# Forgetting attention with two FFN layers on one core: queries' and keys' high parts made in place, copies of the output and the normalising moved within a step

## The chip, the cores and the metric

The program runs on one core of a Trainium2 chip. Times are device microseconds of one execution. Before the change the median of three runs is 1031.77 us (1030.31 to 1033.46). One execution was taken by the hardware profiler; it took 1022.97 us, of which 1021.2 us are the span from its first to its last instruction.

## The reference

Everything is float32. For 4 batches of 8 heads with 576 positions and 64 columns a head:

```python
scores = scale * q @ k.T                       # scale = 1/8
cum = cumsum(log(clip(f, 1e-4, 1)), axis=-1)
scores = where(causal, -1e9, scores + cum[:, :, :, None] - cum[:, :, None, :])
attn = exp(scores - max(scores)); attn = attn / (sum(attn) + 1e-9)
x = (attn @ v) laid out as 2304 tokens x 512
h = x @ w_in;  x = (h - tanh(h)) @ w_out       # first FFN, 512 -> 2048 -> 512
h = x @ w_in2; out = (h * sigmoid(h)) @ w_out2 # second FFN
```

## The kernel before

Float32 accuracy is reached by splitting an operand into a high part that TensorE takes exactly and the rest, `hi` and `lo`, and by summing hi·hi, hi·lo and lo·hi.

**Stages.** The attention of 16 pairs of heads comes first and takes some 237 us of the span; the two FFN layers follow. Of the change only the attention is touched.

**Tiles and steps.** Each pair has nine score tiles: four of the first head (128, 256, 384 and 512 keys), one tile with the last 64 queries of both heads (576 keys), four of the second head. The 144 tiles are numbered through, and one loop goes over a step number n. In step n TensorE transposes tile n - 9, scores tile n + 2 and does a part of the products with the values of an older pair. VectorE takes the row minimum of tile n (`least`), ScalarE the exponential of tile n - 1 (`expo`). Results of a transposition are copied by ScalarE (`evac_a`) and VectorE (`evac_b`). Every third step VectorE sums three rows' sums (`guard`) and GpSimd scales the three finished tiles by the reciprocals (`normalise`). `collect_a`, `collect_b` and `collect_0` copy a head's output from PSUM into x. The order of the calls in the loop (lines 759 to 782) is the order of the instructions on each engine, since the schedule is written by hand. Engines run ahead of each other as far as their semaphores let them.

**The operands of the scores.** Two buffers serve the pairs in turn, pair p the buffer p % 2. A buffer is two tiles, `kqa` and `kqb`, each with one slot for the first and one for the second head. From the third pair on a head's scores are two matmuls: in `kqa` rows 0 to 63 hold hi of keys and queries, rows 64 to 127 hold lo of the keys beside hi of the queries; in `kqb` rows 0 to 63 hold hi of the keys beside lo of the queries, rows 64 to 67 the decay (`dec`). The matmul on `kqb` thus reads the decay rows too. (The first two pairs use the buffers in a plain form, with four matmuls a tile.)

**How they get there.** `load_kq` brings the raw keys and queries of both heads, 128 rows. `split` makes hi (GpSimd the keys, VectorE the queries) and lo (GpSimd, four pieces) in two tiles of their own, `kqhi` and `kqlo`, of which there is one each. `place` then moves them by DMA from SyncE's queue, ten copies of 64 rows a pair and two small ones for the decay. `prep` (line 676) says in which step of a pair each of these calls is issued. SyncE takes its DMAs strictly in order: a wait of one holds back all behind it. A copy's completion is told by a semaphore.

**Beside it** the weights of the FFN are loaded on the same queue (`wload`, in steps 27, 36, 45, 54, 90, 99, 135 and 137) and decoded by all of ScalarE, VectorE and GpSimd.

Of the kernel before, what the change touches and what calls it, by code (L numbers as in the profile page):

```python
# [8 lines left out]
F32R = mybir.dt.float32r  # L9
# [5 lines left out]
P = 128  # L15
B, H, S, D = 4, 8, 576, 64
# [9 lines left out]
K0, Q0, Z1, Q1, W = 64, 64 + S, 64 + S + 512, 128 + S + 512, 192 + S + 512  # L26
RAW = W - K0
# [13 lines left out]
def forgetting_attention_two_ffn(  # L41
# [12 lines left out]
    nc = tc.nc  # L54
# [9 lines left out]
    def rd(ap):  # L64
        return ap.bitcast(F32)
# [140 lines left out]
    for l in range(2):  # L206
        c0 = 0
        for si, nch in enumerate(SETS[l]):
# [8 lines left out]
            for j, n in enumerate(span):  # L217
                a, b = (nxt * NSTAGE * (j + i) // len(span) for i in range(2))
# [109 lines left out]
    def attention():  # L328
        with ExitStack() as actx:
# [4 lines left out]
            def pool(stack, name, bufs=1, **kw):  # L334
                return stack.enter_context(tc.tile_pool(name=name, bufs=bufs, side="right", **kw))
# [9 lines left out]
            rq = pool(earlier, "rq")  # L345
            ps_s = pool(early, "ps_s", 3, space=PSUM)

            NP = B * NPAIR
            raw, vraw, kqs, vals = {}, {}, {}, {}
            kqt = []  # L350
            for i in range(2):
                ta = kp.tile([P, 2, W], F32R, name=f"kqa{i}")
                tb = kp.tile([P, 2, W], F32R, name=f"kqb{i}")
                kqt.append((ta, tb))
# [14 lines left out]
            plain = [[t[:, j, K0:W] for t, j in ((ta, 0), (ta, 1), (tb, 0))] for ta, tb in kqt]  # L369
# [12 lines left out]
            def sub(out, a, b):  # L382
                nc.gpsimd.tensor_tensor(out, a, b, ALU.subtract)

            def split(p, j):
                if p not in kqs:
                    kqs[p] = plain[p][0:2] if p < 2 else [
                        rq.tile([P, RAW], F32R, tag=tag, name=f"{tag}{p}") for tag in ("kqhi", "kqlo")
                    ]
                hi, lo = kqs[p]  # L390
                if j == 0 and p > 1:
                    nc.gpsimd.tensor_scalar(hi[:, 0:S], raw[p][:, 0:S], 1.0, 1.0, ALU.mult, ALU.mult)
                elif j < 2:
                    c = KQ if j == 0 else slice(S, RAW)
                    (nc.vector.tensor_copy if p else nc.scalar.copy)(hi[:, c], raw[p][:, c])
                else:
                    c0, c1 = ((0, 288), (288, S), (S, S + 320), (S + 320, RAW))[j - 2]
                    sub(lo[:, c0:c1], raw[p][:, c0:c1], rd(hi[:, c0:c1]))

            def split_last(p, j):  # L400

# [24 lines left out]
            def place(p, j):  # L426


                ta, tb = (rd(t) for t in kqt[p % 2])
                if j == 2:  # L430
                    src = dec[2 * p:2 * p + 2].rearrange("h r w -> r h w")
                    if p < 4:

                        nc.vector.memset(tb[64:68, :, Z1:Q1], 0.0)
                    nc.sync.dma_start(out=tb[64:68, :, K0:Z1], in_=src[:, :, 0:S + 512])
                    nc.sync.dma_start(out=tb[64:68, :, Q1:W], in_=src[:, :, S + 512:2 * S])
                    return
                for h in range(2):
                    a = rd(kqs[p][j][64 * h:64 * h + 64])
                    if j == 0:  # L440
                        nc.sync.dma_start(out=ta[0:64, h, K0:W], in_=a)  # L441
                        nc.sync.dma_start(out=ta[64:128, h, Q0:W], in_=a[:, S:RAW])  # L442
                        nc.sync.dma_start(out=tb[0:64, h, K0:Q0], in_=a[:, 0:S])
                    else:
                        nc.sync.dma_start(out=ta[64:128, h, K0:Q0], in_=a[:, 0:S])
                        nc.sync.dma_start(out=tb[0:64, h, Q0:W], in_=a[:, S:RAW])

            def prep_v(p, j):
                r = vraw[p].rearrange("p h (c d) -> p c h d", d=D)[:, :, 0, :]
# [82 lines left out]
            def guard(n):  # L532
                sm = rowsum[n // 3] = small.tile([P, 3], F32, tag="sm", name=f"sm{n}")
                nc.vector.tensor_reduce(sm, sums[:, n // 3 % 5], axis=AX.X, op=ALU.add)  # L534

            def normalise(n):
                sm = rowsum.pop(n // 3)
                nc.vector.reciprocal(sm, sm)  # L538
                for j in range(3):
                    pt, w, _ = ptile[tiles[n + j]]  # L540
                    nc.gpsimd.tensor_scalar(pt[:, :w], pt[:, :w], sm[:, j:j + 1], 1.0, ALU.mult, ALU.mult)  # L541
# [7 lines left out]
            def transposes(t):  # L549
                p, h, i = t  # L550
                pt = ptile[t][0] if i == 4 else ptile.pop(t)[0]
                tp = ps_t.tile([P, 4, P], F32, tag="t", name=f"t{p}_{h}_{i}")
                nch = min(i + 1, 4)
                for c in range(nch):
                    nc.tensor.transpose(tp[:, c, :], pt[:, c * P:c * P + P], ident)  # L555
                if i == 4:
                    tps[t] = tuple(
                        [(tp[:, :, 64 * g:64 * g + 64], lambda a: cols(a, 512, 4, 64))] for g in range(2)
                    )
                    return  # L560
                a = [(tp[:, 0:nch, :], lambda a: cols(a, P * i, nch, P))]
                tps[t] = (a, []) if h == 0 else ([], a)
                if (h, i) == (1, 0):

                    t5, o = tp[:, 1, :], 448 * 4 + 512
                    nc.tensor.transpose(t5, ptile.pop((p, 2, 4))[0][:, 512:640], ident)
                    for g in range(2):
                        tps[t][g].append((t5[:, 64 * g:64 * g + 64], lambda a: a[:, o:o + 64]))

            def evac_a(t):  # L570
                ptf = ptfs[t[0] % 2]
                for src, dst in tps[t][0]:
                    nc.scalar.copy(dst(pth), src)  # L573
                for src, dst in tps[t][1]:
                    if t[2] >= 3:
                        nc.scalar.copy(dst(ptf), src)
# [77 lines left out]
            for j in range(2, 6):  # L654
                split(0, j)
            split_last(0, 1)
            dec = dram.tile([BH, 4, 2 * S], F32, name="dec")
# [12 lines left out]
            for a in pt4:  # L670
# [3 lines left out]
            scores(tiles[1])  # L674

            prep = {
                -8: [(load_kq, None)], -5: [(split, 0), (split, 1)], -4: [(split, 2)], -3: [(split, 3)],
                -2: [(split, 4), (place, 2), (place, 0)], -1: [(split, 5), (place, 1)],
                10: [(prep_v, 0)], 12: [(prep_v, 1)], 15: [(load_v, None)],
            }  # L680
            due = {}
# [1 line left out]
            def later(n, fn, *a):  # L683
                due.setdefault(max(n, 0), []).append((fn, a))

            def run(n, *fns):
                for fn, a in due.get(n, []):
                    if fn in fns:
                        fn(*a)

            for p in range(NP - 1):
                for k, items in prep.items():
                    for fn, j in items:
                        if fn is prep_v:
                            later(9 * p + k, fn, p + 1, j)
                        elif j is not None:
                            if p:
                                later(9 * p + k, fn, p + 1, j)
                        elif p + 2 < NP and (p or fn is load_v):
                            later(9 * p + k, fn, p + 2)  # L700

            parts = (
                ([(0, 0), (64, 0), (64, 1)], [(64, 2), (64, 3), (64, 4)]),
# [2 lines left out]
            for n, (p, h, i) in enumerate(tiles):  # L706
# [3 lines left out]
                if (h, i) in ((2, 4), (1, 3)):  # L710
                    h = int(h == 1)
# [13 lines left out]
            def has(n):  # L725
                return 0 <= n < N
# [32 lines left out]
            for n in range(N + LAG + 9):  # L759
                if has(n - LAG):  # L760
                    transposes(tiles[n - LAG])
                if has(n + 2) and tiles[n + 2][2] < 4:
                    scores(tiles[n + 2])
                run(n, scores_tail, values)
                run(n, collect_a)
                if has(n - LAG - 1):
                    evac_a(tiles[n - LAG - 1])
                if has(n - 1):
                    expo(n - 1)
                run(n, collect_b)  # L770
                run(n, collect_0)
                if has(n - LAG - 2):
                    evac_b(tiles[n - LAG - 2])
                if n % 3 == 2 and has(n - 5):
                    guard(n - 5)
                if has(n):
                    least(tiles[n])
                if n % 3 == 2 and has(n - 5):
                    normalise(n - 5)
                run(n, load_kq, load_v, split, place, prep_v)  # L780
                for fn, *a in ahead.get(n - N, []):
                    fn(*a)
# [4 lines left out]
    with tc.manual_schedule():  # L787
        attention()
        for n in range(len(steps) + HL):
            if n > HL:  # L790
                front(n)
            if n >= HL:
                project(n - HL)
# [39 lines left out]
```

## Time and profile before

| what | us |
|---|---|
| median of three runs | 1031.77 |
| profiled execution | 1022.97 |
| its span | 1021.2 |
| span up to 237.3 us (attention) | 237.3 |
| span from there (FFN layers) | 783.9 |
| TensorE busy in these two parts | 211.1 and 780.1 |
| mean busy share of the 16 DMA engines in these two parts | 0.78 and 0.12 |

A busy TensorE is modelled, so what tells more is how far apart the same work of one pair and the next begins. In the rows below PE is TensorE's matmuls, PEld its weight loads, DVE VectorE, ACT ScalarE, POOL GpSimd, and SPq SyncE's queue, on which an instruction's time is that of issuing the DMA, not of its transfer. In the chain of waits a piece named DMA lasts from the start of the issue to the landing that somebody waited for.

### The profile page before, as it was taken

Reading aid. Unit: us, or ns where it says so; the run is one execution under the profiler, and the core shown is the slowest. Engines: PE = TensorE matmul, PEld = TensorE weight load, DVE = VectorE, ACT = ScalarE, POOL = GpSimd, SP = SyncE. Lnnn points to the kernel's source line nnn. Section 1 sums busy time; section 2 is a strip of 40 time slices with the busy share of each in tenths; the row PEclk is TensorE's granted clock in tenths of the full one; section 3 lists DMA queues with packets and bytes.
Section 4 is the critical chain, followed back from the end, with each engine's and each line's share of the span. In section 5 each row is a group of like instructions: output and inputs, shape, how many; then the busy total and the mean of one; then the engine's idle time right before and its main releaser. Section 6 shows DMA issues by size and latency. Waiting matters only on the chain.

```text
span 1021.2 us, 14016 instructions
## 1 busy us (share of the span) xinstructions
PE 991.2 (97%) x4944; PEld 828.5 (81%) x4944; DVE 597.1 (58%) x1385; ACT 492.8 (48%) x1094; POOL 202.1 (20%) x288
## 2 busy tenths in 40 slices
PE   5989989999999999999999999999999999999998
PEld 4777777877898888988888888888888888888887
DVE  6677788878686544757466674443453456633323
ACT  4678788885355342434343444343344334433222
POOL 8677888975000000000000000000000000000000
PEclk9999999999999999999999999999999999999999
DMA  5899999812221101111011220110110111001111
GB/s 154 231 256 258 226 234 268 211 49 84 82 83 42 42 1 42 62 63 42 1 42 49 77 83 1 42 41 21 63 42 1 42 42 42 1 1 42 42 41 62
DMA packets 28181, 81.78 MB, mean 80 GB/s; under 512 B 4368, under 2 KB 4368, under 8 KB 28080
## 3 DMA queue, kind: packets, MB, share of 16 engines
q1 hardware_dynamic: 28104, 80.88, 27.0%
q8 instruction: 39, 0.64, 0.3%
q14 instruction: 30, 0.25, 0.1%
q10 hardware_dynamic: 8, 0.02, 0.0%
HBM read 49.39 MB, written 5.31 MB: 54 GB/s over the span
## 4 chain that ended last, share of the span: by engine, by line
PE 85%; DMA 5%; ACT 3%; SPq 2%; POOL 2%; DVE 2%; issue 1%; DVEq 0%; POOLq 0%; ACTq 0%
PE a L315 39%; PE h L256 38%; PE out_t L600 3%; DMA kqb<-kqhi 2%; PE t L555 2%; PE s L473 2%; DMA vraw<-v 1%; ACT p L527 1%; DMA kqb<-kqlo 1%; SPq L441 1%; POOL p L541 1%; PE s L477 1%; SPq L442 1%; ACT pth L573 1%; PE s L476 1%
## 5 line engine op out<-in xcount | busy, mean ns | idle before, releaser
L256 PE MATMUL h<-xh,wh 128*128 128x512 f32 (+1 forms) x640 | 237.2, 371 | 0.0
L256 PE MATMUL h<-xl,wh 128*128 128x512 f32 (+1 forms) x640 | 235.5, 368 | 0.0
L256 PE MATMUL h<-xh,wl 128*128 128x512 f32 (+1 forms) x640 | 235.5, 368 | 0.0
L278 DVE TENSOR_TENSOR gl<-g,gh 128x512 fp32r<-128x512 f32 (+1 forms) x158 | 101.6, 643 | 101.8 <-ACT gh L274 99.8
L274 ACT CAST gh<-g 128x512 fp32r<-128x512 f32 (+1 forms) x160 | 92.6, 579 | 95.9 <-DVE g L271 93.4
L256 PEld LDWEIGHTS h<-xh,wh 128*128 128x128 f32 x640 | 120.7, 189 | 21.1 <-issue 0.7
L256 PEld LDWEIGHTS h<-xl,wh 128*128 128x128 f32 x640 | 120.7, 189 | 21.0 <-issue 0.7
L256 PEld LDWEIGHTS h<-xh,wl 128*128 128x128 f32 x640 | 120.6, 188 | 20.0
L315 PE MATMUL a<-gh,wh 128*128 128x512 f32 (+1 forms) x320 | 117.9, 369 | 0.0
L315 PE MATMUL a<-gl,wh 128*128 128x512 f32 (+1 forms) x320 | 117.8, 368 | 0.0
L315 PE MATMUL a<-gh,wl 128*128 128x512 f32 (+1 forms) x320 | 117.7, 368 | 0.0
L315 PE MATMUL a<-wh,gh 128*128 128x512 f32 x288 | 112.2, 390 | 0.0
L315 PE MATMUL a<-wl,gh 128*128 128x512 f32 x288 | 112.2, 390 | 0.0
L315 PE MATMUL a<-wh,gl 128*128 128x512 f32 x288 | 112.0, 389 | 0.0
L273 ACT ACTIVATE g<-h 128x512 f32<-128x512 f32 (+1 forms) x80 | 44.4, 555 | 113.6 <-PE h L256 98.5
L244 DVE TENSOR_TENSOR xl<-y,xh 128x512 fp32r<-128x512 f32 (+1 forms) x60 | 37.4, 638 | 96.6 <-ACT xh L242 96.6
L242 ACT CAST xh<-y 128x512 fp32r<-128x512 f32 (+1 forms) x60 | 34.2, 580 | 104.8 <-PE h L256 103.1
L527 ACT ACTIVATE p<-p,mn 128x128 f32<-128x128 f32 (+3 forms) x128 | 72.3, 565 | 9.7 <-DVE mn L511 4.8
L541 POOL TENSOR_SCALAR p<-p,sm 128x128 f32<-128x128 f32 (+3 forms) x128 | 69.9, 558 | 22.9 <-DVE sm L538 10.4
L555 PE MATMUL t<-ident,p 128*128 128x128 f32 x320 | 59.6, 285 | 12.7 <-DVE sm L534 9.2
L244 DVE TENSOR_TENSOR xl<-x,xh 128x512 fp32r<-128x512 f32 (+1 forms) x56 | 34.5, 634 | 62.2 <-ACT xh L242 62.2
L315 PEld LDWEIGHTS a<-gh,wh 128*128 128x128 f32 x320 | 60.3, 189 | 10.4 <-ACT x L611 0.4
(127 smaller groups left out, 1690.8 us busy)
## 6 DMA issues: line engine op xcount, KB each, us to landing
raw<-w_in SPq DMA_DIRECT2D x32, 512.0 KB
raw<-w_out SPq DMA_DIRECT2D x32, 512.0 KB
kqraw<-kq SPq DMA_DIRECT2D x16, 608.0 KB
kqa<-kqhi SPq DMA_DIRECT2D x28, 304.0 KB
vraw<-v SPq DMA_DIRECT2D x16, 320.0 KB
out<-ob SPq DMA_DIRECT2D x18, 256.0 KB
kqa<-kqhi SPq DMA_DIRECT2D x28, 160.0 KB
kqb<-kqlo SPq DMA_DIRECT2D x28, 160.0 KB
```

Source lines behind the costliest of these rows:

```text
L242: nc.scalar.copy(hi[:, :n], src[:, k, t0:t0 + n])
L244: eng.tensor_tensor(lo[:, :n], src[:, k, t0:t0 + n], rd(hi[:, :n]), ALU.subtract)
L256: nc.tensor.matmul(hp[:, :n], w[:, k * P:k * P + P], m[:, :n], start=(k == 0 and r == 0), stop=(k == NKT - 1 and r == 2),)
L273: nc.scalar.activation(g[:, :n], hp[:, :n], AF.Silu)
L274: nc.scalar.copy(gh[:, :n], g[:, :n])
L278: eng.tensor_tensor(gl[:, :n], g[:, :n], rd(gh[:, :n]), ALU.subtract)
L315: nc.tensor.matmul(dst, w, m, start=(first and r == 0), stop=(last and r == 2))
L473: nc.tensor.matmul(s[:, :n], a[:, q], b[:, 0:n], start=r == 0, stop=r == 3)
L527: nc.scalar.activation(pt[:, :w], pt[:, :w], AF.Exp, bias=mn, scale=-1.0, accum_out=sums[:, n // 3 % 5, n % 3, 0:1],)
L541: nc.gpsimd.tensor_scalar(pt[:, :w], pt[:, :w], sm[:, j:j + 1], 1.0, ALU.mult, ALU.mult)
L555: nc.tensor.transpose(tp[:, c, :], pt[:, c * P:c * P + P], ident)
L600: nc.tensor.matmul(dst, w, pt[:, 448 * c + a:448 * c + q1], start=(c == 0 and r == 0), stop=(c == last and r == len(terms) - 1),)
```

## The change

There are three parts.

- **Copies of the output.** In a step `collect_a` and `collect_b` go behind `evac_a`, `expo`, `evac_b`, `guard` and `least`.
- **Normalising.** The reciprocal goes into `guard`, directly behind the sum; the scaling on GpSimd is issued one step later.
- **Operands.** hi is written by `split` directly into slot 0 of `kqa`, all 128 rows, where the first head's 64 rows are in place. lo of the queries goes into slot 0 of `kqb`; lo of the keys goes into one tile `klo`. `place` has eight copies instead of ten, now in three groups: four copies of hi, then the two of `klo`, then two more of queries; the second group overwrites rows that the first one reads, and the third frees the rows into which the decay goes, which is now last. Splits and copies of the third and fourth pair are issued three steps later, since these replace buffers in plain form.

```diff
             def split(p, j):
-                if p not in kqs:
-                    kqs[p] = plain[p][0:2] if p < 2 else [
-                        rq.tile([P, RAW], F32R, tag=tag, name=f"{tag}{p}") for tag in ("kqhi", "kqlo")
-                    ]
-                hi, lo = kqs[p]
+                ta, tb = kqt[p % 2]
+                if p > 1:
+                    hi, lo = ta[:, 0, K0:W], (klo, tb[:, 0, Q0:W])
+                else:
+                    hi, lo = plain[p][0], (plain[p][1][:, 0:S], plain[p][1][:, S:RAW])
...
             def place(p, j):
...
+                moves = (
+                    ((ta[top, 1, K0:W], ta[end, 0, K0:W]), (ta[end, 1, qs], ta[end, 0, qs]),
+                     (tb[top, 1, kk], ta[end, 0, kk]), (tb[top, 0, kk], ta[top, 0, kk])),
+                    ((ta[end, 1, kk], rd(klo[end])), (ta[end, 0, kk], rd(klo[top]))),
+                    ((tb[top, 1, qs], tb[end, 0, qs]), (ta[end, 0, qs], ta[top, 0, qs])),
+                )
+                if j < 3:
+                    for a, b in moves[j]:
+                        nc.sync.dma_start(out=a, in_=b)
                     return
-                for h in range(2):
-                    a = rd(kqs[p][j][64 * h:64 * h + 64])
-                    if j == 0:
-                        nc.sync.dma_start(out=ta[0:64, h, K0:W], in_=a)
-                        nc.sync.dma_start(out=ta[64:128, h, Q0:W], in_=a[:, S:RAW])
-                        nc.sync.dma_start(out=tb[0:64, h, K0:Q0], in_=a[:, 0:S])
-                    else:
-                        nc.sync.dma_start(out=ta[64:128, h, K0:Q0], in_=a[:, 0:S])
-                        nc.sync.dma_start(out=tb[0:64, h, Q0:W], in_=a[:, S:RAW])
...
             def guard(n):
...
+                nc.vector.reciprocal(sm, sm)
...
             prep = {
-                -8: [(load_kq, None)], -5: [(split, 0), (split, 1)], -4: [(split, 2)], -3: [(split, 3)],
-                -2: [(split, 4), (place, 2), (place, 0)], -1: [(split, 5), (place, 1)],
+                -8: [(load_kq, None)], -5: [(split, 0), (split, 1)], -4: [(split, 2)],
+                -3: [(split, 3), (split, 4)], -2: [(split, 5), (place, 0)], -1: [(place, 1)],
+                0: [(place, 2), (place, 3)],
...
                             if p:
-                                later(9 * p + k, fn, p + 1, j)
+                                later(9 * p + k + (3 if p < 3 else 0), fn, p + 1, j)
...
                 run(n, scores_tail, values)
-                run(n, collect_a)
                 if has(n - LAG - 1):
                     evac_a(tiles[n - LAG - 1])
                 if has(n - 1):
                     expo(n - 1)
-                run(n, collect_b)
-                run(n, collect_0)
                 if has(n - LAG - 2):
                     evac_b(tiles[n - LAG - 2])
                 if n % 3 == 2 and has(n - 5):
                     guard(n - 5)
                 if has(n):
                     least(tiles[n])
-                if n % 3 == 2 and has(n - 5):
-                    normalise(n - 5)
+                run(n, collect_a)
+                run(n, collect_b)
+                run(n, collect_0)
+                if n % 3 == 0 and has(n - 6):
+                    normalise(n - 6)
```

SyncE's queue before, for one pair in the middle of the attention, from the second of its decay's rows to the load of the next raw keys and queries (kqhi and kqlo are the split parts, 64x1216 is a head's keys and queries, 64x640 its queries, 64x576 its keys):

```order
42 L436 DMA kqb_103<-dec 4x2x64
43 L441 DMA kqa_102<-kqhi_608 64x1216
44 L442 DMA kqa_102<-kqhi_608 64x640
45 L443 DMA kqb_103<-kqhi_608 64x576
46 L441 DMA kqa_102<-kqhi_608 64x1216
47 L442 DMA kqa_102<-kqhi_608 64x640
48 L443 DMA kqb_103<-kqhi_608 64x576
49 L445 DMA kqa_102<-kqlo_609 64x576
50 L446 DMA kqb_103<-kqlo_609 64x640
51 L445 DMA kqa_102<-kqlo_609 64x576
52 L446 DMA kqb_103<-kqlo_609 64x640
53 L141 DMA raw_0_0_724<-w_in 128x1024
54 L375 DMA kqraw_740<-kq 128x1216
```

The decay (dec) goes ahead of a pair's ten copies, and the loads for later pairs follow the copies. The same queue after the change, from a weight load and the two loads ahead of a pair to that pair's end:

```order
41 L141 DMA raw_0_0_713<-w_in 128x1024
42 L377 DMA kqraw_729<-kq 128x1216
43 L382 DMA vraw_827<-v 128x640
44 L446 DMA kqa_105<-kqa_105 64x1216
45 L446 DMA kqa_105<-kqa_105 64x640
46 L446 DMA kqb_106<-kqa_105 64x576 x2
47 L446 DMA kqa_105<-klo 64x576 x2
48 L446 DMA kqb_106<-kqb_106 64x640
49 L446 DMA kqa_105<-kqa_105 64x640
50 L452 DMA kqb_106<-dec 4x2x1088
51 L453 DMA kqb_106<-dec 4x2x64
```

The decay's two rows moved from the head of a pair's copies to their end, and the loads for the next pair stand directly behind them.

GpSimd before, over the same part of a pair (p are finished tiles being scaled, kqhi and kqlo the split):

```order
71 L392 TENSOR_SCALAR kqhi_801<-kqraw_547 128x576
72 L541 TENSOR_SCALAR p_0_0_721<-p_0_0_721,sm_817 128x128
73 L541 TENSOR_SCALAR p_0_1_735<-p_0_1_735,sm_817 128x256
74 L541 TENSOR_SCALAR p_0_2_759<-p_0_2_759,sm_817 128x384
75 L383 TENSOR_TENSOR kqlo_802<-kqraw_547,kqhi_801 128x288 x2
76 L383 TENSOR_TENSOR kqlo_802<-kqraw_547,kqhi_801 128x320
77 L541 TENSOR_SCALAR p_0_3_782<-p_0_3_782,sm_890 128x512
78 L541 TENSOR_SCALAR pt_1_107<-pt_1_107,sm_890 128x576
79 L541 TENSOR_SCALAR p_1_0_819<-p_1_0_819,sm_890 128x128
80 L383 TENSOR_TENSOR kqlo_802<-kqraw_547,kqhi_801 128x320
```

And after:

```order
71 L396 TENSOR_SCALAR kqa_105<-kqraw_599 128x576
72 L385 TENSOR_TENSOR klo<-kqraw_599,kqa_105 128x288
73 L548 TENSOR_SCALAR p_0_0_701<-p_0_0_701,sm_804 128x128
74 L548 TENSOR_SCALAR p_0_1_723<-p_0_1_723,sm_804 128x256
75 L548 TENSOR_SCALAR p_0_2_748<-p_0_2_748,sm_804 128x384
76 L385 TENSOR_TENSOR klo<-kqraw_599,kqa_105 128x288
77 L385 TENSOR_TENSOR kqb_106<-kqraw_599,kqa_105 128x320 x2
78 L548 TENSOR_SCALAR p_0_3_768<-p_0_3_768,sm_872 128x512
79 L548 TENSOR_SCALAR pt_1_108<-pt_1_108,sm_872 128x576
80 L548 TENSOR_SCALAR p_1_0_807<-p_1_0_807,sm_872 128x128
```

The first piece of lo moved ahead of three scalings, the last piece ahead of three more; the number of instructions is the same.

## Rows read from the trace of the kernel before

**Rows 1.** The page: the span.
```profile
span 1021.2 us, 14016 instructions
```

**Rows 2.** Busy time by stretch; the last columns are granted clock, DMA share, GB/s.
```profile
0.00:237.30 237.30, 211.09 (x1237) 171.68 (x1237) 180.54 (x665) 182.28 (x533) 193.99 (x283) 0.99 0.78 207
237.30:1021.20 783.90, 780.13 (x3711) 656.79 (x3709) 416.56 (x721) 310.56 (x562) 8.09 (x6) 1.00 0.12 42
...
49.30:189.66 140.36, 128.37 (x804) 105.93 (x804) 111.99 (x443) 114.68 (x350) 116.24 (x171) 0.99 0.93 243
60.00:80.00 20.00, 17.21 (x111) 14.10 (x110) 14.05 (x60) 15.44 (x47) 15.45 (x25) 1.00 0.98 262
...
180.00:200.00 20.00, 19.89 (x129) 16.34 (x128) 16.56 (x68) 17.57 (x54) 19.75 (x28) 1.00 0.81 196
```

**Rows 3.** Chain of waits of 18 to 240 us: start, us, what.
```profile
49.30 0.94 PE out_t L600 x4
...
88.79 0.96 PE out_t L600 x4
141.00 0.95 PE out_t L600 x4
178.26 0.94 PE out_t L600 x4
...
189.66 0.95 PE out_t L600 x4
...
201.05 0.96 PE out_t L600 x4
```

**Rows 4.** Who waited for whom up to 240 us: total us, times, longest.
```profile
PE t L555 <- DVE sm L534: 9.2, 9, 1.8
POOL kqhi L392 <- DMA kqb<-kqhi: 7.6, 4, 3.0
ACT tmp L615 <- PE out_t L600: 16.0, 15, 2.1
```

**Rows 5.** The tile kqraw: durations of its readers, and what their engine's idle time ended with.
```profile
L395 DVE CAST kqhi<-kqraw x14: 487/494/2252, 20.2 to 186.5; 128x640 fp32r<-128x640 f32 x14
  DMA kqb<-kqhi: 10.2, 7
  DMA kqa<-kqlo: 4.6, 2
  DMA kqa<-kqhi: 3.7, 3
```

**Rows 6.** SyncE's queue in order of time: start, us of issue.
```profile
37.09 0.27 SPq L435 DMA_DIRECT2D kqb<-dec  x1
...
37.82 0.47 SPq L441 DMA_DIRECT2D kqa<-kqhi  x1
38.33 0.60 SPq L442 DMA_DIRECT2D kqa<-kqhi  x1
```

**Rows 7.** The same chain as rows 3: DMAs from issue to landing.
```profile
79.92 4.89 DMA kqb<-kqhi
118.42 3.48 DMA kqb<-kqhi
161.34 3.31 DMA kqb<-kqlo
```

**Rows 8.** The program's start in order of time: first loads and their readers.
```profile
0.74 0.39 SPq L633 DMA_DIRECT2D x<-f  x1
1.19 0.88 SPq L375 DMA_DIRECT2D kqraw<-kq  x2
2.69 0.96 DVE L112 TENSOR_SCALAR x<-x 32x576 f32<-32x576 f32 x1
5.46 0.67 ACT L395 CAST kqa<-kqraw 128x576 fp32r<-128x576 f32 x1 [1.10 <-DMA kqraw<-kq]
```

**Rows 9.** One wait of ScalarE near the end of the attention.
```profile
203.39 0.58 ACT L615 COPY tmp<-out_t 64x512 f32<-64x512 f32 x1 [0.64 <-PE out_t L600]
```

More of the change, by code (lines that the diff above doesn't have):

```diff
@@ L348, in attention @@
             NP = B * NPAIR
-            raw, vraw, kqs, vals = {}, {}, {}, {}
+            raw, vraw, vals = {}, {}, {}
             kqt = []
+            klo = rq.tile([P, S], F32R, name="klo")
             for i in range(2):
@@ L397, in split @@
                     c0, c1 = ((0, 288), (288, S), (S, S + 320), (S + 320, RAW))[j - 2]
-                    sub(lo[:, c0:c1], raw[p][:, c0:c1], rd(hi[:, c0:c1]))
+                    b = S * (j > 3)
+                    sub(lo[j > 3][:, c0 - b:c1 - b], raw[p][:, c0:c1], rd(hi[:, c0:c1]))
             def split_last(p, j):
@@ L429, in place @@
                 ta, tb = (rd(t) for t in kqt[p % 2])
[L430 to L436, printed above, removed]
-                    return
-                for h in range(2):
-                    a = rd(kqs[p][j][64 * h:64 * h + 64])
-                    if j == 0:
-                        nc.sync.dma_start(out=ta[0:64, h, K0:W], in_=a)
-                        nc.sync.dma_start(out=ta[64:128, h, Q0:W], in_=a[:, S:RAW])
-                        nc.sync.dma_start(out=tb[0:64, h, K0:Q0], in_=a[:, 0:S])
-                    else:
-                        nc.sync.dma_start(out=ta[64:128, h, K0:Q0], in_=a[:, 0:S])
-                        nc.sync.dma_start(out=tb[0:64, h, Q0:W], in_=a[:, S:RAW])
+                top, end = slice(0, 64), slice(64, 128)
+                kk, qs = slice(K0, Q0), slice(Q0, W)
+                moves = (
[7 more added lines that the diff above has]
+                        nc.sync.dma_start(out=a, in_=b)
+                    return
+                src = dec[2 * p:2 * p + 2].rearrange("h r w -> r h w")
+                if p < 4:
+                    nc.vector.memset(tb[64:68, 1, Z1:Q1], 0.0)
+                nc.sync.dma_start(out=tb[64:68, :, K0:Z1], in_=src[:, :, 0:S + 512])
+                nc.sync.dma_start(out=tb[64:68, :, Q1:W], in_=src[:, :, S + 512:2 * S])
             def prep_v(p, j):
@@ L534, in guard @@
                 nc.vector.tensor_reduce(sm, sums[:, n // 3 % 5], axis=AX.X, op=ALU.add)
+                nc.vector.reciprocal(sm, sm)
             def normalise(n):
                 sm = rowsum.pop(n // 3)
-                nc.vector.reciprocal(sm, sm)
                 for j in range(3):
@@ L697, in attention @@
                             if p:
-                                later(9 * p + k, fn, p + 1, j)
+                                later(9 * p + k + (3 if p < 3 else 0), fn, p + 1, j)
                         elif p + 2 < NP and (p or fn is load_v):
-                            later(9 * p + k, fn, p + 2)
+                            later(9 * p + k + (3 if fn is load_kq and p < 4 else 0), fn, p + 2)
             parts = (
```

## The prediction

> **What bounds the kernel now.** I read four views: the busy time by stretch, the chain of waits, who waits for whom, and SyncE's queue. The second table row says where not to look: from 237.3 us on TensorE is busy 780.13 of 783.9 us [rows 2], and the change touches nothing there. So only the attention can move the time, 237 us of a span of 1021.2 [rows 1].
>
> In the attention the reader should look at one mark that comes once a pair, the first product with the values behind a pair's first scores [rows 3]. From 178.26 to 189.66 to 201.05 us it is 11.40 and 11.39 us apart, and TensorE is busy 19.89 of 20 us there while the DMA engines are at 0.81 [rows 2]. That is TensorE's own pace: 11.4 us a pair. From 49.30 to 189.66 there are eleven pairs in 140.36 us, 12.76 each; at 11.4 they would take 125.4. So 15.0 us are lost, and that is all that can be won in this stretch. The same stretch shows the DMA engines at 0.93 with 243 GB/s [rows 2]; from 60 to 80 us they are at 0.98 with 262 GB/s. The bytes agree: kq 608 KB, v 320 and ten copies (304 + 160 + 144 + 144 + 160 for each head, 1824) are 2752 KB a pair, and six weight loads of 512 KB fall into the stretch, 34.1 MB in all, at 243 GB/s the 140 us.
>
> A second cause lies beside it. VectorE's split waits until copies have left the one `kqhi` tile (10.2 + 4.6 + 3.7 = 18.5 us of idle time [rows 5]), GpSimd's likewise (7.6 us), and TensorE's transpositions wait 9.2 us for VectorE [rows 4].
>
> **The operands.** Two copies go, hi of the first head (64x1216, 304 KB) and lo of its queries (64x640, 160 KB), which are made in place: 464 KB of 1824, 17% of a pair's 2752; at 260 GB/s 1.8 us of transfer. The split's wait for `kqhi` goes too: it now waits for TensorE's last use of slot 0, a third of a pair earlier. Instructions of VectorE and GpSimd stay as many; the order of GpSimd has lo's first pieces earlier. What is late next is the copies themselves, since they have become a series. Name them in their order: four of hi (304, 160, 144, 144 KB), two of `klo`, two of queries. SyncE takes its queue in order. The second `klo` copy overwrites what the first and third read and waits until these have landed; the decay overwrites what the first query copy reads and waits for that; and behind the decay stand the weight load, the next kq and v, and the next pair's copies. Before, ten copies were issued back to back, 0.5 to 0.6 us each [rows 6], and nothing in the queue waited for a landing.
>
> I follow one turn, from the issue of one pair's decay to that of the next:
> - two decay issues, 37.09 to 37.82: 0.73 us [rows 6]
> - the kq load from issue to its first reader, nothing ahead of it: 1.19 to 5.46, 4.25 us [rows 8]
> - v and the first three copies behind it, 320 + 304 + 160 + 144 = 928 KB. The engines move 243 GB/s at a share of 0.93 and 262 at 0.98 [rows 2], some 260 when busy: 3.65 us. TensorE must be through with the pair before last when the first copy goes; that is at the landing of the decay, while kq is still on its way, so it costs nothing
> - the second `klo` copy's issue, 0.60 us [rows 6]
> - the first query copy (160 KB) from issue to landing. Not shown alone; from below the smallest load at the start, 0.74 to 2.69 or 1.95 us [rows 8], and its own 0.63 us of bytes, 2.6; from above 3.31 us, the same form with others ahead [rows 7]. I take the middle, 2.9
>
> The sum is 12.1 us a pair. With a weight load in front, 512 KB more at 260 GB/s, 2.0 us: 14.1. The weights fall into steps 27, 36, 45, 54, 90 and 99, one pair each, so 5 × 12.1 + 6 × 14.1 = 145.1 us in place of 140.36: 4.7 us more. TensorE's pace (11.4) lies below both, so it hides nothing, and its wait moves to each pair's first scores. The 15 us that the lighter traffic could give back are lost to the series.
>
> The fourth pair's start, three steps later: its first copy can go no earlier than now (37.82 [rows 6]), the third follows 1.1 us later and lands 3.5 after that [rows 7], + 0.6 + 2.9, and the decay lands after 2.6 more, at 48.5 us; the mark is at 49.30 now. I put 0.2 us on it.
>
> Ends of the sum. Below: 2.6 for the query copy and nothing else less, 11.8 and 13.8, 141.8 us, +1.4. Above: kq at 4.89, the longest landing of a copy in the chain [rows 7], bytes at 243 GB/s (3.91 and 2.16), the query copy 3.31: 13.4 and 15.6, 160.6 us, +20.2.
>
> The Trainium skill ("DMA: Bandwidth & Descriptors", section "Anatomy of one DMA — SWDGE (gpsimd) path") gives a DMA about 2.0 us fixed plus its bytes at 436 GB/s. Its fit is for GpSimd's queue, and this one is SyncE's; by it kq would take 3.4 us, the 928 KB 2.2, the query copy 2.4, and a turn 9.3, an estimate by that page. The trace has 262 GB/s at a share of 0.98, so I don't go by it.
>
> **The output's copies and the normalising.** ScalarE's copy of an output waits for TensorE 15 times, 16.0 us in all, up to 2.1 [rows 4], with the evacuation of transposed tiles and an exponential queued behind it. At the back of the step these go first. While TensorE waits for DMAs that costs or gives nothing; after the last loads it may give what ScalarE's wait shows there, 0.64 us [rows 9]. I take -0.7 us; ends are 0 and, if two of the last three pairs have it, -1.3. The reciprocal stays on VectorE with its instructions around it, and GpSimd scales tile n - 6 in step n while TensorE transposes it in step n + 3: nothing, covered by three steps (some 3.8 us at 11.4 a pair); if that cover went, TensorE's transpositions would wait for GpSimd.
>
> Sum: 4.7 + 0.2 - 0.7 = +4.2 us. The profiled execution took 1022.97 us, 1021.2 of it span; the median of the runs shown is 1031.77, so 8.8 us lie between executions. I add the difference to the median: **1036 us**; own range 1032 (+1.4 - 1.3) to 1045 (about two thirds of the way to the upper end).
>
> **The rivals.**
> - *The bytes decide* (faster). If the transfers of one pair overlap what the next needs so that a turn fits under 11.4 us, weights included, the marks fall at TensorE's pace: -15.0 + 0.2 - 0.7, 1016 us. For it: the engines' share of 0.93 to 0.98 and 17% fewer bytes. Against: 0.73 + 4.25 + 0.60 + 2.6 are 8.2 us before a byte of v or of a copy is counted. (The Trainium skill's figures above would give this case, 9.3 us and 10.5 with a weight load.)
> - *The weights hide* (faster). From 49.30 to 88.79 three pairs with three weight loads take 13.16 us each; from 88.79 to 141.00 four with one take 13.05 [rows 3]. So a load need not lengthen its pair. At 12.1 throughout, 133.1 us: -7.3 + 0.2 - 0.7, 1024 us. Against: before, a pair's loads filled a wait for `kqhi`; now they stand in the series.
> - *Loaded prices* (slower still): the upper end, 13.4 and 15.6: 1051 us. It decides if kq and the copies land as late as now under load (4.89 [rows 7]).
> - *The output's bank*: the copies at the step's end keep TensorE from its next product with the values, 0.3 us (half of the wait in rows 9) on 15 pairs: 1040.5 us. Against: now ScalarE waits for TensorE there, not the other way.
>
> **How the numbers follow.** What a measurement of this kernel can tell from no change is some 0.3%, 3.1 us: faster is below 1028.7, slower above 1034.9. My forecast has 0.47 (same 0.15, slower 0.32), the bytes 0.20 (faster), the weights hidden 0.17 (faster 0.14, same 0.03), loaded prices 0.11 and the output's bank 0.05 (slower). Faster 0.34, same 0.18, slower 0.48. The range goes from 1016, the bytes' case, to 1046; outside lie half of that case and most of the loaded prices.
>
> **What would show it.** In the profile after: marks some 12.1 us apart without and 14.1 with a weight load; the wait of a pair's first scores ended by the decay's landing; SyncE's queue waiting at the second `klo` copy and at the decay, on landings; the split's wait for copies gone; a lower DMA share (near 0.8) in the stretch. Marks 11.4 us apart would refute the series, a weight load that leaves its pair's length as it is would refute the term of 2.0 us, and waits of TensorE for the output's copies would show the last rival.

## The result, and the profile after

The change made the kernel slower: 1043.73 us median of four runs (1036.38 to 1046.34) against 1031.04 for the kernel before, a ratio of 1.0142 with a 95% interval of 1.0099 to 1.0185 (ratios are those on record for the runs; the two medians alone give 1.0123). Forecast was 1036, a loss of 4.2 us, with a range of 1016 to 1046; measured is 12.7 us. The profiled execution took 1046.34 us, the longest of the four, and that of the kernel before, 1022.97, was shorter than any of the other three there. So the two profiles, 23.3 us apart in span [rows 1], show more loss than the medians. An execution over 1.5% longer than the fastest of its kernel counts as slow, and two of the medians below leave one such execution out (1048.28 and 1645.75 us). The FFN layers are as they were: the last 783.9 us have TensorE busy for 780.13 us in both. All of the difference is in the attention.

First the busy time by stretch (columns as in [rows 2]: stretch, PE, PEld, DVE, ACT, POOL, granted clock, DMA share, GB/s), of the kernel after:

```profile
49.30:189.66 140.36, 124.38 (x710) 103.34 (x710) 100.17 (x390) 102.66 (x309) 101.27 (x152) 0.92 0.73 185
80.00:90.00 10.00, 9.84 (x54) 8.62 (x55) 5.13 (x20) 7.57 (x22) 6.18 (x10) 0.83 0.85 214
90.00:100.00 10.00, 7.70 (x37) 6.47 (x36) 6.03 (x27) 5.37 (x17) 6.30 (x10) 0.76 0.75 215
180.00:190.00 10.00, 7.27 (x30) 6.22 (x30) 4.75 (x22) 4.92 (x15) 6.47 (x10) 0.70 0.78 215
```

Against the same stretch before (0.93, 243 GB/s, clock 0.99) the DMA engines are less busy, at 0.73 and 185 GB/s, and yet TensorE does 710 matmuls in it instead of 804. So the engines are no longer at work throughout. The turn of SyncE's queue from 122.57 to 136.85 us, whose rows follow below, shows where they stand still. Their share is 0.29 up to 124.50, 0.98 with 256 GB/s from there to 131.00, 0.26 up to 133.00, 0.92 up to 135.00 and 0.15 to the end. Bytes still fill the middle of a turn; the idle stretches ahead of the landings are new. The granted clock is lower too: 0.92 over the stretch, down to 0.70 in ten microseconds.

The marks, once a pair, in the chain of waits (start, us, what) with two of the DMAs in it:

```profile
42.21 1.76 PE out_t L607 x4
...
54.94 0.95 PE out_t L607 x4
...
66.81 0.94 PE out_t L607 x4
...
111.21 0.96 PE out_t L607 x4
...
140.17 0.96 PE out_t L607 x4
...
177.47 4.05 DMA kqb<-kqb
181.54 2.64 DMA kqb<-dec
185.14 1.76 PE out_t L607 x4
...
213.29 0.95 PE out_t L607 x4
...
224.69 0.95 PE out_t L607 x4
```

The row at 54.94 is the mark at 49.30 of [rows 3], 5.6 us later. From it to 213.29 are the eleven pairs that took 140.36 us: 158.35 now, 14.4 each. The last, 11.40 apart, is at TensorE's pace again. At 185.14 four matmuls that otherwise take 0.95 us take 1.76, after a wait for the copies and the decay; that stretch has the clock of 0.70.

SyncE's queue in order of time (start, us of issue; one that waits counts from when it may go, but rows that are merged hold the wait between them):

```profile
108.08 0.28 SPq L452 DMA_DIRECT2D kqb<-dec  x1
...
108.91 0.36 SPq L141 DMA_DIRECT2D raw<-w_out  x1
109.31 0.43 SPq L377 DMA_DIRECT2D kqraw<-kq  x1
...
113.69 6.19 SPq L446 DMA_DIRECT2D kqa<-klo  x2
119.97 0.55 SPq L446 DMA_DIRECT2D kqb<-kqb  x1
...
122.57 0.28 SPq L452 DMA_DIRECT2D kqb<-dec  x1
...
123.23 0.36 SPq L377 DMA_DIRECT2D kqraw<-kq  x1
...
127.77 4.78 SPq L446 DMA_DIRECT2D kqa<-klo  x2
132.64 0.55 SPq L446 DMA_DIRECT2D kqb<-kqb  x1
...
136.85 0.28 SPq L452 DMA_DIRECT2D kqb<-dec  x1
```

One turn runs from decay to decay: 14.49 us with a weight load (108.08 to 122.57), 14.28 without (122.57 to 136.85). The eleven turns from 49.21 to 209.84 us take 160.63 us: the five without a weight load 13.15 to 15.04, 13.9 in the mean, the six with one 14.32 to 16.29, 15.2 in the mean. The long issue of the `klo` pair is the first landing that is waited for; the gap behind the query copy (119.97 to 122.57, 132.64 to 136.85) is the second. Before, these rows stood 0.5 to 0.6 us apart [rows 6].

Who waited, SyncE's queue up to 255 us (total us, times, longest):

```profile
SPq L446 <- DMA kqb<-kqa: 39.5, 14, 6.1
...
SPq L452 <- DMA kqb<-kqb: 22.2, 14, 3.0
...
SPq L446 <- DMA kqa<-kqa: 11.4, 4, 3.7
```

And the engines, same stretch:

```profile
PE s L484 <- DMA kqb<-dec: 13.1, 9, 2.0
...
POOL klo L385 <- DMA kqa<-klo: 11.4, 8, 2.5
...
PEld s L484 <- DMA kqb<-dec: 6.9, 5, 2.1
```

These are 14 pairs. The second `klo` copy waits for the third copy in each, and in four of them for the first copy before that, so the first landing costs the queue 3.6 us a pair (39.5 + 11.4) and the second 1.6. TensorE waits at first scores for the decay. VectorE's split waits for no copy any more, but GpSimd's does: in place of `kqhi` [rows 4] it now waits until copies have left the one `klo` tile, 11.4 us in eight waits. The queue itself hardly waits for TensorE: between 60 and 200 us some 4.6 us in all, against 57.3 for landings of copies.

### The profile page after: what moved, and what is told of

Its sections match the earlier page's. It is cut to its first block, busy times and chain, and to the rows that moved or that the text cites. A ratio compares the mean times of both kernels' runs of the same rounds, so it can differ in the third digit from the quotient of the medians.

```text
span 1044.5 us, 13926 instructions
## 1 busy us (share of the span) xinstructions
PE 1008.1 (97%) x4944; PEld 843.0 (81%) x4944; DVE 601.2 (58%) x1385; ACT 494.5 (47%) x1094; POOL 200.7 (19%) x288
## 4 chain that ended last, share of the span: by engine, by line
PE 85%; DMA 7%; POOL 3%; ACT 2%; DVE 2%; issue 1%; SPq 0%; POOLq 0%; ACTq 0%; DVEq 0%
PE a L315 38%; PE h L256 37%; PE out_t L607 3%; DMA kqb<-kqb 2%; DMA kqb<-kqa 2%; DMA kqb<-dec 2%; PE t L562 2%; PE s L480 2%; POOL p L548 1%; PE s L484 1%; DVE x L632 1%; ACT p L534 1%; ACT ptf L583 1%; ACT tmp L622 1%; DMA kqa<-klo 0%
## 5 line engine op out<-in xcount | busy, mean ns | idle before, releaser
L534 ACT ACTIVATE p<-p,mn 128x128 f32<-128x128 f32 (+3 forms) x128 | 72.1, 563 | 10.2 <-DVE mn L518 9.8
L518 DVE CUSTOM_DVE_ANT_0 p<-s,mask 128x128 f32<-128x128 f32 (+3 forms) x128 | 61.6, 482 | 25.2 <-PE s L484 17.2
```

Of the source, the lines that this page charges most:

```text
L518: nc.vector.tensor_tensor_reduce(out=pt[:, c0:c0 + src.shape[1]], in0=src, in1=m, op0=ALU.add, op1=ALU.min, scale=-SCALE, scalar=init, acc ...
L534: nc.scalar.activation(pt[:, :w], pt[:, :w], AF.Exp, bias=mn, scale=-1.0, accum_out=sums[:, n // 3 % 5, n % 3, 0:1],)
```

## The experiments

Theories: **series** (each pair's copies became a chain of landings in one queue, and that chain is longer than TensorE's pace) against **order** (the moved output copies and normalising hold engines up) and **bytes** (transfers set the pair's length, as they did before). Each was timed in turn with the kernel before on the same chip, another chip for each of three groups; the medians of the kernel before were 1028.83 us for the first four, 1027.11 for the next four and 1028.20 for the last two. Across groups the ratios are what to compare.

**The parts alone.** The operands without the other two parts, and the other two on the kernel before:

```diff
# operands alone: the loop of the kernel before
                 run(n, scores_tail, values)
+                run(n, collect_a)
...
-                if n % 3 == 0 and has(n - 6):
-                    normalise(n - 6)
+                if n % 3 == 2 and has(n - 5):
+                    normalise(n - 5)
```

> The operands' part alone: hi made in place, eight copies in three groups; the output's copies and the normalising stand where they stood before. If the series of copies (kq, v, four copies, a landing, the query copy, a landing, the decay) is the whole cost, the time is that of the full change, 1044 us (1036 to 1048), with marks 13 to 16 us apart while raw keys and queries are still loaded. If the moved output copies and normalising carry the loss (ScalarE and GpSimd later in a step), this one comes back to 1031 us (1026 to 1034).

> The other part alone, on the kernel before: output's copies at the step's end, reciprocals in the sum's step, the scaling a step later; ten copies as before. The series theory says 1031 us, 0 to 1 us less than before (the 0.7 us of the prediction). The rival that the output's bank or the scaling a step later holds TensorE up says 1036 us or more, with waits of TensorE for ScalarE's or VectorE's copies of out_t, or for the scaling.

Measured: operands alone 1041.73 us, ratio 1.0118 (1.0050 to 1.0186); the other parts alone 1029.19, ratio 0.9996 (0.9963 to 1.0028). The loss is the operands', and the order is worth nothing that can be measured. The stretch of operands alone looks like the full change, 0.75 and 185 GB/s:

```profile
49.30:189.66 140.36, 121.60 (x708) 98.99 (x707) 96.66 (x385) 99.35 (x306) 99.97 (x151) 0.94 0.75 185
```

**One landing less.** The query copy, which waits for nothing of the first group, goes ahead of the `klo` copies:

```diff
-    ((ta[end, 1, kk], rd(klo[end])), (ta[end, 0, kk], rd(klo[top]))),
-    ((tb[top, 1, qs], tb[end, 0, qs]), (ta[end, 0, qs], ta[top, 0, qs])),
+    ((tb[top, 1, qs], tb[end, 0, qs]), (ta[end, 1, kk], rd(klo[end])), (ta[end, 0, kk], rd(klo[top]))),
+    ((ta[end, 0, qs], ta[top, 0, qs]),),
```

> The changed kernel with one copy moved: the second head's lo queries (64x640) go ahead of the two klo copies in place of behind them, so that the decay no longer waits for a landing of its own; bytes and everything else unchanged. The series theory: 2.0 us a pair less (a copy's issue and landing, 2.6, less what the third group's last copy takes), 14.3 to about 12.3 us a pair, 11 pairs and the ends 22 to 25 us less: 1020 us (1016 to 1028), the kernel before or better. The rival that transfer time or the loads' bytes set the pair's length: no change, 1042 us (1036 to 1046).

Measured: 1024.11 us, ratio to the kernel before 0.9972 (0.9931 to 1.0013). The same copies and bytes, one row of the queue in another place: 17.6 us less than operands alone on the same chip (15.0 by the two ratios), 19.6 less than the full change by its own runs (17.5 by the ratios). That shows the series, since only the query copy's place was changed. GpSimd's wait for `klo` is still there, 8.9 us in seven waits where it was 11.4 in eight, so the loss didn't hang on it. The queue, one turn without a weight load:

```profile
113.92 0.48 SPq L452 DMA_DIRECT2D kqb<-dec  x1
...
120.28 0.46 SPq L446 DMA_DIRECT2D kqb<-kqb  x1
120.80 4.35 SPq L446 DMA_DIRECT2D kqa<-klo  x2
125.24 0.98 SPq L446 DMA_DIRECT2D kqa<-kqa  x1
126.27 0.48 SPq L452 DMA_DIRECT2D kqb<-dec  x1
```

The decay follows the last copy at once; the turn is 12.35 us, not 14.28. The DMA engines have more to do in the same time, 0.83 and 211 GB/s:

```profile
49.30:189.66 140.36, 133.23 (x825) 110.51 (x824) 116.76 (x448) 117.86 (x355) 117.22 (x174) 0.99 0.83 211
```

The clock is back at 0.99 there. What the clock cost in the full change isn't separated: it fell where TensorE waited, and that went with the waits. Nor is a lower clock the operands' alone: the profile of the other parts alone, at 1028.85 us, has 0.95 in the same stretch with the DMA engines at 0.91.

**Fewer bytes, no series.** Is the premise right that bytes bounded the kernel before?

```diff
# before; h is the head
-    nc.sync.dma_start(out=ta[0:64, h, K0:W], in_=a)
+    if h or p < 4:
+        nc.sync.dma_start(out=ta[0:64, h, K0:W], in_=a)
...
-    nc.sync.dma_start(out=tb[0:64, h, Q0:W], in_=a[:, S:RAW])
+    if h or p < 4:
+        nc.sync.dma_start(out=tb[0:64, h, Q0:W], in_=a[:, S:RAW])
```

> The kernel before with the first head's hi (64x1216) and lo queries (64x640) not copied from the fifth pair on: 464 KB a pair less in the same back-to-back queue, so no series. The output of these pairs is not the reference's. If bytes bounded the kernel before, as the rival of the prediction has it, the pairs come near TensorE's 11.4 us and the time near 1019 us (1015 to 1024). If the wait of the split for the kqhi tile bounds it beside the bytes, part of the 15 us stays: 1024 to 1029 us.

Measured: 1016.27 us, ratio 0.9879 (0.9825 to 0.9933). So the two copies that the change saves, here left out from the fifth pair on, were worth 12.6 us, most of the 15 us that I counted, if nothing had been put in their place. Their bytes and their two places in the queue went together and aren't told apart. The idle time ahead of the split of `kqraw` fell with them (VectorE and GpSimd until a DMA of `kqhi`, total us, times; 10.2 + 4.6 + 3.7 before in [rows 5]):

```profile
  DMA kqb<-kqhi: 3.0, 1
```

So the wait for the `kqhi` tile, still a single buffer, went with the two copies. Whether it was a cause of its own beside the bytes this run can't tell, since fewer copies also leave the tile earlier.

**The early pairs.** The third and fourth pair made as before (`kqhi`, `kqlo`, ten copies, no delay), the series elsewhere:

```diff
+                early_prep = {
+                    -8: [(load_kq, None)], -5: [(split, 0), (split, 1)], -4: [(split, 2)], -3: [(split, 3)],
+                    -2: [(split, 4), (place, 3), (place, 0)], -1: [(split, 5), (place, 1)],
...
-                for k, items in prep.items():
+                for k, items in (early_prep if p < 3 else prep).items():
```

> The changed kernel, but the third and fourth pair are made as in the kernel before (split into kqhi and kqlo, ten copies, no three steps' delay); the series stays for the other twelve. In the profile of the change the fourth pair's first scores come 5.6 us later than before. If the delayed copies and the hi made in place cause that, it goes: 1038 us (1034 to 1042), first scores of the fourth pair at 48 to 50 us. If it is the clock of TensorE in the first 45 us, which the later steps share, it stays or comes and goes from run to run: 1043 us.

Measured: 1038.21 us, ratio 1.0107 (1.0005 to 1.0209), too wide to tell from the full change. The trace tells more. The third pair's first scores still come at 41.24 us, and TensorE is slow ahead of them; in the run with all three edits, which has the same code for these pairs, they come at 36.71. The last plain score and the first in the new form (start, us), in the one and in the other:

```profile
39.88 0.62 PE L494 MATMUL s<-kqb 64*128 64x512 f32 x1
41.24 0.41 PE L498 MATMUL s<-kqb 68*128 68x128 f32 x1
```

```profile
35.94 0.39 PE L494 MATMUL s<-kqb 64*128 64x512 f32 x1
36.71 0.28 PE L498 MATMUL s<-kqb 68*128 68x128 f32 x1
```

The same matmul takes 0.62 or 0.39 us. That does not follow from the early pairs' code: operands alone, which has the delayed steps, has 0.39 too, and the full change 0.62. It follows from when TensorE becomes fast after the start, which the last section shows. Of the profiles set beside each other here, those of the full change, of this run, of the query copy ahead and of the weights moved have 0.62 still at 40 us, and the seven others 0.39 before 37. All four late ones have the change's operands, and so have three of the seven early ones; whether the operands make a late one more frequent isn't shown.

**More on the shorter series.** Four runs on top of the query copy ahead, each with an edit of its own. The output's copies and normalising where they stood before:

> The query copy ahead of the klo copies, and the output's copies and the normalising back where they stood before the change. If these moves are worth nothing also where the series is shorter: 1024 us (1019 to 1028), the same as with them. If they help once TensorE is nearer its own pace, as the prediction's 0.7 us has it or more: 1025 to 1028 us. If they hurt (they come with the late first scores of the third pair at 41 us in two profiles, and not in the two profiles without both parts): 1018 to 1021 us.

Measured: 1026.82 us, ratio 1.0009 (0.9972 to 1.0046), against 0.9972 (0.9931 to 1.0013) with them. The intervals overlap; a gain of up to a few microseconds from the moves isn't excluded, a loss isn't seen.

The weight loads between the two `klo` copies (they are issued a step earlier, and the second `klo` copy goes from the second group of `place` into the third; the first edit is shown):

```diff
-    ((27, 0, 0), (36, 0, 1), (45, 1, 0), (54, 1, 1), (90, 2, 0), (99, 2, 1),
+    ((26, 0, 0), (35, 0, 1), (44, 1, 0), (53, 1, 1), (89, 2, 0), (98, 2, 1),
```

> The query copy ahead of the klo copies, and besides each of the six weight loads stands between the two klo copies, where SyncE waits for a landing anyway, not behind the decay in front of the raw keys. If a weight load adds its 1 to 2 us to a pair only because it lies in the series: pairs with weights come from about 13 us to 11.4 to 12, 6 x 1 to 1.5 us less, 1017 us (1012 to 1021). If its bytes count wherever they stand (the transfers alone fill the pair): the same as without, 1024 us (1020 to 1028).

Measured: 1024.47 us, ratio 0.9989 (0.9953 to 1.0025): no gain. The wait for the landing halved, from 24.3 to 11.8 us, and the wait of the values' load for TensorE grew by a little more, 14.6 us (SyncE's queue; first with the query copy ahead alone, then with the weights moved):

```profile
SPq L446 <- DMA kqb<-kqa: 24.3, 12, 3.8
SPq L382 <- PE out_t L607: 18.4, 9, 4.4
```

```profile
SPq L382 <- PE out_t L607: 33.0, 13, 4.6
...
SPq L446 <- DMA kqb<-kqa: 11.8, 10, 2.4
```

All three edits:

> All three: query copy ahead, weight loads between the klo copies, third and fourth pair made as in the kernel before. If the parts add: 1012 us (1008 to 1017), below both kernels; if the early part gives nothing, the time of the run with the first two, 1017 to 1024.

Measured: 1023.16 us, ratio 0.9961 (0.9931 to 0.9991). The parts don't add.

A fourth buffer for the values instead:

```diff
-    vraw[p] = vp.tile([P, 2, 5 * D], F32, tag="vraw", name=f"vraw{p}", bufs=3)
+    vraw[p] = vp.tile([P, 2, 5 * D], F32, tag="vraw", name=f"vraw{p}", bufs=4)
```

> The query copy ahead of the klo copies, and a fourth buffer for the raw values, so that SyncE's load of the values doesn't wait for TensorE's last product with older ones (18 us in nine waits in the run with the query copy ahead, and all of the next pair's copies stand behind that load). If these waits lengthen pairs: 1019 us (1013 to 1022), the waits of line 382 gone. If they lie beside the wait of the first copy for TensorE's scores: 1024 us (1020 to 1028).

Measured: 1022.89 us, ratio 0.9939 (0.9911 to 0.9968): the best ratio among the kernels that leave nothing out, though its interval overlaps that of three buffers. The wait of line 382 is gone, and the first copy now waits for TensorE's scores:

```profile
SPq L446 <- PE s L483: 26.5, 10, 5.0
SPq L446 <- DMA kqb<-kqa: 18.3, 10, 4.1
```

**Bytes saved without a series.** On the kernel before, one cast of VectorE in place of the 64x1216 copy of the first head's hi:

```diff
-    nc.sync.dma_start(out=ta[0:64, h, K0:W], in_=a)
+    if h:
+        nc.sync.dma_start(out=ta[0:64, h, K0:W], in_=a)
+    else:
+        nc.vector.tensor_copy(kqt[p % 2][0][0:64, 0, K0:W], raw[p][0:64])
```

> The kernel before with one copy less and no series: the first head's hi is made a second time, by VectorE straight into its 64 rows of kqa, in place of the 64x1216 copy (304 KB of 1824 a pair; VectorE gets one cast of 64x1216 a pair, about 0.9 us). If bytes bounded the kernel before, as the run with 464 KB fewer shows, two thirds of its 12 us come: 1021 us (1017 to 1025). If VectorE's added 0.9 us a pair or its longer wait takes it back: 1027 us or more.

Measured: 1022.65 us, ratio 0.9966 (0.9937 to 0.9994), a gain of 3.5 us by the ratio and 5.6 by the medians, with 304 KB less a pair and no landing waited for. VectorE's busy time in the stretch went up from 111.99 us [rows 2] to 126.31:

```profile
49.30:189.66 140.36, 130.41 (x807) 107.18 (x806) 126.31 (x455) 115.64 (x352) 120.43 (x171) 0.99 0.84 221
```

## Why the prediction was right, and which terms were too small

The mechanism was the one that was forecast. The operands' part lost time and the series did it. Of the signs that the prediction named, these are there: SyncE waits at the second `klo` copy and at the decay, TensorE waits at first scores, VectorE's split waits for no copy, and the DMA share fell (0.73 where 0.8 was said). GpSimd's split still waits, for `klo` in place of `kqhi`, and the turns are longer than was said. The direction and the range held; the size did not, 12.7 us where 4.2 was worked out.

That the time fell into the range is in part luck. The turns of the profile are those of the rival *Loaded prices*, which had a chance of 0.11: it had 13.4 and 15.6 us and 160.6 in all, and 13.9, 15.2 and 160.6 were measured. From profile to profile the loss is 23.3 us, which on the median before would be beyond the range; the medians are only 12.7 us apart.

*The turn.* The sum priced a turn in pieces. The trace of the change has every DMA's landings, sixteen for each load and each copy, of which the last counts here. Over the eleven turns from 49.21 to 209.84 us (five without a weight load, six with one):

| piece | forecast, us | mean, us | least to most |
|---|---|---|---|
| turn without a weight load | 12.1 | 13.9 | 13.15 to 15.04 |
| turn with a weight load | 14.1 | 15.2 | 14.32 to 16.29 |
| kq from issue to landing, no weight load | 4.25 | 4.85 | 3.88 to 7.11 |
| from there to the landing of the third copy, all turns | 3.65 | 4.7 | 3.69 to 5.56 |
| query copy's issue to the decay's issue, all turns | 2.9 | 3.06 | 2.60 to 4.21 |

So the term for the 928 KB behind kq was 1.0 us too small and that for kq 0.6. One rate, 260 GB/s for everything, is the weak point: in the turn from 122.57 us the engines moved 296 GB/s from 126 to 128 us (kq and v) and 209 to 246 from 128 to 131 (the rest of v, and the copies), at shares of 0.97 to 1.03.

*The query copy.* Forecast 2.9, between 2.6 and 3.31. The mean is near it; three of eleven turns lie above the upper bound, and why these do isn't shown. The Trainium skill ("DMA: Bandwidth & Descriptors", section "Anatomy of one DMA — SWDGE (gpsimd) path"), with some 2.0 us fixed and bytes at 436 GB/s, would give this copy 2.4 us, an estimate by that page for another queue; the trace's 2.60 is near it for a copy with nothing much ahead, and its 4.05 and 4.21 are not.

*The weight load.* Forecast 2.0 us on its pair; the turns with one are 1.25 us longer in the mean. From 111 to 113 us, where the weights and kq are on their way, the engines moved 345 to 358 GB/s, more than the 260 of the sum. That the weights' place doesn't matter was shown where the series is shorter (ratio 0.9989 against 0.9972), not in the full change.

*A term that was missing.* TensorE waits each pair, and its granted clock fell to 0.92 in the stretch (0.99 before). The sum took TensorE's pace as 11.4 us whatever it had waited. How much of the 18 us that the stretch grew by comes from it was not separated. What it can have added to the turns directly is small, since the queue waited for TensorE only some 4.6 us between 60 and 200 us.

*The early pairs.* Forecast 0.2 us; the profile has 5.6. The matmuls ahead of the third pair take 1.6 times as long there as in other runs of the same code, so this is not the delayed copies but TensorE's later rise to its fast pace (last section). It is in the profiled execution, and how often in the others can't be read.

*The rest.* The output's copies and the normalising: forecast -0.7 us; measured alone, 0.4 us slower than the kernel before by the medians and as much faster by the ratio, with an interval of 3 us to either side, which is none that can be told. The rival of the output's bank fell with that run. The rival that the bytes decide was right on the kernel before (12.6 us for 464 KB a pair) and wrong on the change: the bytes were saved, and the time went into landings. *Loaded prices*, 1051 us, was too much for the median, though not for the turns of the profile. One reading of the prediction was double: the 18.5 us of idle time [rows 5] are VectorE's and GpSimd's together, with GpSimd's 7.6 among them; no term of the sum used it.

## What to carry to other kernels

Copies that overwrite each other's sources in one in-order queue wait for landings, and whatever stands behind them waits too, loads for the next round included; count a round from landing to landing and compare it with the pace of the engine that it feeds, before counting the bytes saved. Within such a series look first for a copy that waits for nothing and put it ahead: here that was worth 15 to 20 us, more than the two saved copies (12.6). When a wait is removed look what takes its place: the weights' move only moved the waiting to the values' load, and a fourth buffer moved that to TensorE's scores.

## What the runs showed that was not expected

- TensorE's clock fell in the attention of a kernel that is 97% busy over its span: granted 0.70 from 180 to 190 us after a wait of the pair's first scores (4.05 and 2.64 us of landings in the chain), where four matmuls took 1.76 us instead of 0.95. Of the two levels, 2.4 and 1.2 GHz, a mean of 0.70 means 6 of the 10 us at the lower one.
- In the first 45 us the granted clock reads 1.00 in the profiles of the change and of operands alone, and it isn't to be believed there: the trace's record of the clock begins at 44.2 us in the profile of the change and at 32.2 in that of operands alone. What TensorE did before shows in the same matmul (64x512). In the kernel before it took 0.62 us at 28.20 and 0.39 at 36.63, so TensorE started slow and became fast in between; in the change it still took 0.62 at 40.06. Four products with the values took 1.76 us at 42.21, as at 185.14, where the clock was at the lower of its levels, and 0.95 otherwise. So by these durations TensorE ran at the lower level from the start, in the profile of the change some 12 us longer, which accounts for the 5.6 us of the early pairs. Why it rose later there stays open.

The kernel before:

```profile
28.20 0.62 PE L473 MATMUL s<-kqb 64*128 64x512 f32 x1
...
36.63 0.39 PE L473 MATMUL s<-kqb 64*128 64x512 f32 x1
```

The change, and operands alone:

```profile
40.06 0.62 PE L480 MATMUL s<-kqb 64*128 64x512 f32 x1
```

```profile
36.30 0.39 PE L480 MATMUL s<-kqb 64*128 64x512 f32 x1
```

- The wait for a single buffer (`kqhi`, 18.5 us in all) fell to 3.0 us when two of the ten copies that read the split parts were left out, with the buffer still single.
